# Sums of a router pass in one operation, buffer clearing moved behind the first casts, an inner loop in the overflow path

## The chip, the cores and the metric

One Trainium2 chip, of which the kernel uses one core. The metric is the device time of one execution in microseconds (us); the time of a kernel is the median of several runs. The core has five engines that run side by side, each with its own queue, in order: TensorE (PE, matmul), VectorE (DVE), ScalarE (ACT), GpSimd (POOL) and SyncE (SP, which here only issues transfers). They wait for each other through semaphores. Transfers (DMA) are issued from the queues of SP, ACT and POOL.

## The reference

```python
# attention: q, k, v (8, 8, 576, 64)
scores = q @ k^T / 8
gamma  = 1 - 2 ** (-5 - head)
D      = where(i >= j, gamma ** (i - j), 0)
x      = ((scores * D) @ v)            # -> x (4608, 512)
# mixture of 8 experts, two of them for each of the 4608 rows
noisy  = x @ w_gate + log1p(exp(x @ w_noise)) * noise
top2   = two largest of noisy in each row
w      = exp(l - max(l)) over these two, divided by their sum
out[row] += w * (relu(x[row] @ w1[e]) @ w2[e])   # for both experts e of the row
```

## The kernel before

**Attention.** 16 units (`u`): a unit is four heads of one batch; four units make a pair of batches (`bp`, 0 to 3). The main loop runs `n` from 0 to 16 and works on unit n and, for the outputs, on unit n-1. SP loads q, k and v of unit n+4 at step n (L172, L177); the loads go into buffers that rotate by four. The last 64 rows of both batches of a pair, the tail, are loaded apart (`load_tail`, L184, tile rawt). `cast` scales k and q by the decay tables and turns them into bfloat16 (kn L195, qb L203) and casts v (vn L200, on ACT). Units 0 and 1 are cast by DVE ahead of the loop, all others by POOL, two steps ahead. PE transposes q and k (L245), ACT evicts them (QT, KT L247), PE computes scores (L260), DVE multiplies them by a triangular mask (S L265, St L337 for the tail), PE computes states (T L284, evicted into Tb L290) and outputs (x L310, L318, evicted into xT L324).

**Router.** When a pair of batches is done, `route(bp)` handles its 1152 rows (128 partitions x C = 9 columns). It is a generator: the main loop takes one piece of it between parts of the attention (`step`, `piece`), and this sets the order on every engine's queue, since the whole stage is under a schedule written out by hand. A pass: logits on PE (R L507), softplus on ACT, top two with DVE (L534 to L566: M has a one for each of the two experts, [P, C, 2, E]), then the counts. `thr` (L572, L573) is the capacity of the chosen expert, `py` (L576, L578) its first row in the buffer, each a product with M and a sum over the E experts. PE sums M over the earlier rows (L604 to L612); `prf` adds the base of the earlier pairs (L617). `rk` (L618, L621) is the row's place among the rows of the same expert and slot, `rc` (L623 to L626) among both slots. From these follow the overflow flag `ov` (L642, L643), the payload `pl` that POOL builds (L593 to L598, L627, L644, L645) and copies beside x (L648), from where SP stores x and payload in `xd` (L650); and the list of rows by expert, through one-hot tiles olo and oh (L665 to L672, PE L682) into `xi`. In SP's queue the stores L650 of a pass stand ahead of the loads of the following steps.

**Experts.** `early` (L386 to L411) computes five tiles of 256 rows as soon as two or three pairs are routed, interleaved with the last attention steps and the last routing pass. `experts` does the other 35: gather by indirect DMA (L841), transposes (L948), first matmul (L964), relu (L969, L971), second matmul (L984), then the first expert's weighted rows to `yd` (L1015), and the sum with them to `out` (L1025, scatter L1031). `load_weights` (L1094, L1097) loads the first two experts' weights through POOL's queue at steps 11 to 14.

**Overflow.** Rows beyond an expert's capacity are handled in `overflow`, a loop that runs `nov` times, a number computed on the chip; all engines load it (L752) and branch (L753). Its body finds the rows of a block with 72 one-hot tiles `oh` (L773) and 72 matmuls into `pL` (L774), written out one after the other.

**Head.** DVE clears the four Tb tiles (L163), sets the constants ones, ltri, mask, maskt (L56 to L85, which POOL then cuts to triangles), copies iota and local into PSUM (L452, L454) and clears base and atleast, all ahead of its first cast.

Of the kernel before, what the change touches and what calls it, by code (L numbers as in the profile page):

```python
# [10 lines left out]
F32 = mybir.dt.float32  # L11
BF16 = mybir.dt.bfloat16
I32 = mybir.dt.int32
AX = mybir.AxisListType.X
Alu = mybir.AluOpType
Act = mybir.ActivationFunctionType

P = 128
N = 4608
NCOL = N // P  # L20
E = 8
# [7 lines left out]
HPE = CAP // P  # L29
# [15 lines left out]
HD = 64  # L45
# [5 lines left out]
def constants(nc, cp):  # L51
    K = {}
    K["ident"] = cp.tile([P, P], BF16, name="ident")
    make_identity(nc, K["ident"])
    K["ones"] = cp.tile([P, P], BF16, name="ones")
    nc.vector.memset(K["ones"], 1.0)  # L56
    K["ltri"] = cp.tile([P, P], BF16, name="ltri")
    nc.vector.memset(K["ltri"], 1.0)
    nc.gpsimd.affine_select(K["ltri"], K["ltri"], pattern=[[1, P]], base=0, channel_multiplier=-1,
                            compare_op=Alu.is_gt, fill=0.0)  # L60
# [12 lines left out]

    K["mask"] = cp.tile([P, 2, P], BF16, name="mask")
    nc.vector.memset(K["mask"], 1.0)
    for h in range(2):
        for rs in range(2):
            m = K["mask"][h * HD:(h + 1) * HD, rs, :].rearrange("p (r q) -> p r q", r=4)
            nc.gpsimd.affine_select(m, m, pattern=[[1, 4], [4, 32]], base=-rs, channel_multiplier=-2,
                                    compare_op=Alu.is_ge, fill=0.0)  # L80
    K["maskt"] = cp.tile([P, 2, HD], BF16, name="maskt")
    nc.vector.memset(K["maskt"], 0.0)
    for b in range(2):
        m = K["maskt"][b * HD:(b + 1) * HD, b, :]
        nc.vector.memset(m, 1.0)  # L85
        nc.gpsimd.affine_select(m, m, pattern=[[1, HD]], base=0, channel_multiplier=-1,
                                compare_op=Alu.is_ge, fill=0.0)
# [5 lines left out]
    for h in range(2):  # L93
        t = K["tok"][h * HD:(h + 1) * HD]
# [38 lines left out]
class Attention:  # L133
# [26 lines left out]
    def tables(self):  # L160
        self.kg, self.qg, self.tg = decay_tables(self.nc, self.cp, self.bf)
        for t in self.Tb:
            self.nc.vector.memset(t, 0.0)  # L163
# [23 lines left out]

    def cast(self, u, eng=None):

        nc = self.nc  # L190
        d = self.u[u]
        eng = eng or nc.gpsimd
        hq = self.unit(u)[1]
        kn = self.bf.tile([P, 2, 2, 4, HD], BF16, name="kn", bufs=3)
        eng.tensor_tensor(kn.rearrange("p r c h d -> p (c h) r d"),  # L195
                                d.pop("rawk").rearrange("p c h (r d) -> p (c h) r d", r=2),
                                self.kg[:, hq].rearrange("p c h r -> p (c h) r").unsqueeze(3).to_broadcast(
                                    [P, 8, 2, HD]), Alu.mult)
        vn = self.bf.tile([P, 2, 2, 4, HD], BF16, name="vn", bufs=3)
        nc.scalar.activation(vn.rearrange("p r c h d -> p (c h) r d"),  # L200
                             d.pop("rawv").rearrange("p c h (r d) -> p (c h) r d", r=2), Act.Copy)
        qb = self.bf.tile([P, 4, 4, HD], BF16, name="qb")
        eng.tensor_tensor(qb.rearrange("p r h d -> p h r d"),  # L203
                                d.pop("rawq").rearrange("p c h w -> p (c h w)").rearrange(
                                    "p (h r d) -> p h r d", h=4, r=4),
                                self.qg[:, hq].unsqueeze(3).to_broadcast([P, 4, 4, HD]), Alu.mult)
        d.update(kn=kn, vn=vn, qb=qb)
# [227 lines left out]
class Router:  # L435
    def __init__(self, tc, ctx, K, at, wgn, moe_noise, xd, keep):
        self.tc, self.nc, self.K, self.at = tc, tc.nc, K, at
        self.wgn, self.xd, self.keep = wgn, xd, keep
        nc = self.nc
# [12 lines left out]
        nc.vector.tensor_copy(self.iota, K["iota"])  # L452
        self.local = bank[:, 368:368 + NC9]
        nc.vector.tensor_copy(self.local, K["local"])  # L454

        self.base = self.one.tile([P, 2, E], F32, name="base")
        nc.vector.memset(self.base, 0.0)
        self.atleast = {}
        for n in (2, 3):
            t = self.atleast[n] = self.one.tile([P, 2, E], F32, name=f"atleast{n}")  # L460
# [14 lines left out]
    def route(self, bp):  # L475

        nc, K, sp = self.nc, self.K, self.sp
        V = nc.vector
        ps = self.at.ps
        C = NC9  # L480
# [24 lines left out]
        for c in range(C):  # L505
            for di in range(KD):
                nc.tensor.matmul(pg[:, c].rearrange("p s e -> p (s e)"), lhsT=xcol(c, di),  # L507
                                 rhs=self.wgn[:, di].rearrange("p s e -> p (s e)"), start=(di == 0), stop=(di == KD - 1))
# [15 lines left out]
        def col(name):  # L524
            return sp.tile([P, C], F32, name=name)
# [30 lines left out]
        w = sp.tile([P, 2, C], F32, name="w")  # L556
        V.tensor_tensor(w[:, 0], w1, w2, Alu.max)
        V.tensor_tensor(w[:, 1], w1, w2, Alu.min)
        SH = [P, C, 2, E]
        M = sp.tile(SH, BF16, name="M")  # L560
# [4 lines left out]
        d = col("d")  # L565
# [4 lines left out]
        pd = sp.tile(SH, F32, name="pd", bufs=1)  # L570
        thr = sp.tile([P, C, 2], F32, name="thr")
        V.tensor_mul(pd, M, K["cap"][:, 0:2].unsqueeze(1).to_broadcast(SH))  # L572
        V.tensor_reduce(thr, pd, AX, Alu.add)  # L573
        yield
        row(5)
        V.tensor_mul(pd[:, :, 0], M[:, :, 0], K["cap"][:, 2].unsqueeze(1).to_broadcast([P, C, E]))  # L576
        py = col("py")
        V.tensor_reduce(py, pd[:, :, 0], AX, Alu.add)  # L578
# [13 lines left out]
        G = nc.gpsimd  # L592
# [4 lines left out]
        G.tensor_scalar(pl[:, :, 0], w[:, 1], -1.0, float(E), Alu.mult, Alu.add)  # L597
        G.tensor_copy(pl[:, :, 3], K["tok"][:, bp])  # L598
# [19 lines left out]
        V.tensor_mul(pd, M, prf)  # L618
        yield
        rk = sp.tile([P, C, 2], F32, name="rk")  # L620
        V.tensor_reduce(rk, pd, AX, Alu.add)  # L621
        prs = sp.tile([P, C, E], F32, name="prs", bufs=1)
        V.tensor_add(prs, prf[:, :, 0], prf[:, :, 1])  # L623
        V.tensor_mul(pd, M, prs.unsqueeze(2).to_broadcast(SH))
        rc = sp.tile([P, C, 2], F32, name="rc")
        V.tensor_reduce(rc, pd, AX, Alu.add)  # L626
# [27 lines left out]
        V.tensor_copy(hi, lh[:, 1])  # L654
        e10 = sp.tile([P, 2, C], F32, name="e10")
        V.tensor_scalar(e10, w, -float(HPE), float(HPE * E), Alu.mult, Alu.add)
        V.tensor_add(hi, hi, e10)
# [88 lines left out]
def overflow(tc, K, w1, w2, keep, xd, yd, out):  # L746
# [3 lines left out]
    with tc.tile_pool(name="ov_c", bufs=1) as cp, tc.tile_pool(name="ov_o", bufs=4) as op, \  # L750
         tc.tile_pool(name="ov_ps", bufs=1, space=bass.MemoryType.PSUM) as ps:
        n = nc.values_load(keep["nov2"][0:1, 0:1], min_val=0, max_val=NOV)  # L752
        with tc.For_i(0, n, 1) as iv:  # L753
# [10 lines left out]
            vals = cp.tile([P, 2, NCOL, 3], BF16, name="vals")  # L764
            for j in range(2):
                V.tensor_copy(vals[:, j, :, 0], K["pidx"].to_broadcast([P, NCOL]))
                V.tensor_copy(vals[:, j, :, 1], K["cols"])
                V.memset(vals[:, j, :, 2], float(j))
            pL = ps.tile([P, 3], F32, name="pL")
            for j in range(2):  # L770
                for c in range(NCOL):
                    oh = op.tile([P, P], BF16, name="oh")
                    V.tensor_scalar(oh, K["iota"], rel[:, j, c:c + 1], None, Alu.is_equal)  # L773
                    nc.tensor.matmul(pL, lhsT=oh, rhs=vals[:, j, c, :], start=(j == 0 and c == 0),  # L774
                                     stop=(j == 1 and c == NCOL - 1))
            L = cp.tile([P, 3], F32, name="L")
            V.tensor_copy(L, pL)
# [324 lines left out]
def kernel(  # L1102
# [27 lines left out]
    with ExitStack() as actx, tc.manual_schedule(engines=order):  # L1130
# [38 lines left out]
        at.tr(0, "k")  # L1169
        at.cast(1, nc.vector)  # L1170
        for n in range(NU + 1):
# [101 lines left out]
```

## Time and profile before

| | |
|---|---|
| five runs | 495.59, 496.13, 497.38, 494.50, 493.87 us; median 495.59 |
| profiled execution | 500.35 us, of it the span from the first to the last instruction 498.7 us |
| PE | 412.9 us busy (83%) |
| VectorE | 242.3 us (49%), 642 instructions |
| ScalarE | 275.8 us (55%) |
| GpSimd | 268.6 us (54%), 346 instructions |
| granted PE clock | 0.91 of full speed in the mean |
| DMA | 104.21 MB, 209 GB/s in the mean |

The busy shares are means over stages that differ. Read by stage: up to 54 us the input loads run without a pause and the engines wait for them; from 54 to 171 us attention and three routing passes run on all engines at once; from 171 to 218 us PE does the early expert tiles while the fourth pass runs; from 218.8 to 480.7 us PE does the 35 other tiles, 7.39 us each; the last scatter lands at 485.5, and the rest of the span is the way past the overflow loop and the end of the program. A line of a timeline gives the start in us, the duration in us, engine, line, operation, output<-inputs, shapes, and in brackets the idle time before it and what ended it.

### The profile page before, as it was taken

To read this page: it belongs to the slowest core of one execution; us is meant where nothing else is said; L and a number is where in the kernel's file an instruction comes from. 1 tells how busy PE (TensorE), PEld (TensorE's weight loads), DVE (VectorE), ACT (ScalarE), POOL (GpSimd) and SP (SyncE) were. 2 spreads that over 40 slices of the span, in tenths; PEclk is the share of its full clock that TensorE was granted. 3 is DMA by queue.
4 is the path that set the end of the run, shared out by engine and by line. 5 is a ranking of instruction groups with operands and counts; after the bars stand their busy time and mean duration, and the time that the engine had idled before them with its cause. 6 is when DMAs were issued, how large, how long until landed. Compare 5 with 4: busy or idle time off the path is not lost.

```text
span 498.7 us, 11756 instructions
## 1 busy us (share of the span) xinstructions
PE 412.9 (83%) x4688; PEld 300.1 (60%) x4688; DVE 242.3 (49%) x642; ACT 275.8 (55%) x405; POOL 268.6 (54%) x346
## 2 busy tenths in 40 slices
PE   0763378697677599989999999999999999999950
PEld 0652367576566467657766766766766766766620
DVE  4531068849867729624334444435345445445240
ACT  3770689678658357554657656655655643322200
POOL 3760734834953423485155717637657777776440
PEclk9987597768777899989999999999999999999985
DMA  8999992797795812573786886887978946545330
GB/s 242 284 266 203 273 288 49 222 300 148 207 219 122 185 44 101 172 244 131 253 253 227 270 305 234 295 290 240 332 268 272 338 138 203 170 141 186 111 126 5
DMA packets 92858, 104.21 MB, mean 209 GB/s; under 512 B 22135, under 2 KB 69752, under 8 KB 92800
## 3 DMA queue, kind: packets, MB, share of 16 engines
q1 hardware_dynamic: 77040, 70.04, 47.7%
q0 software_dynamic: 14176, 32.83, 23.1%
q8 instruction: 38, 0.62, 0.5%
q10 hardware_dynamic: 1584, 0.56, 0.4%
q14 instruction: 20, 0.16, 0.1%
HBM read 84.66 MB, written 28.72 MB: 227 GB/s over the span
## 4 chain that ended last, share of the span: by engine, by line
PE 65%; DVE 11%; DMA 7%; SPq 7%; ACT 4%; issue 2%; POOL 1%; POOLq 0%; ACTq 0%; DVEq 0%
PE p L964 25%; PE po L984 24%; DMA raw_v<-in_v_dram 3%; SPq L177 3%; PE pt L948 3%; PE x L405 3%; DVE S L265 3%; PE T L395 2%; PE S L395 2%; SPq L184 1%; DMA raw_k<-in_k_dram 1%; DMA rawt_k<-in_k_dram 1%; DVE olo L665 1%; DMA rawt_v<-in_v_dram 1%; PE S L260 1%
## 5 line engine op out<-in xcount | busy, mean ns | idle before, releaser
L964 PE MATMUL p<-xgT,w 128*128 128x256 bf16 x1120 | 212.9, 275 | 0.0
L984 PE MATMUL po<-w,hT 128*128 128x512 bf16 x560 | 209.8, 379 | 0.0
L964 PEld LDWEIGHTS <-w 128*128 128x128 bf16 x1120 | 110.4, 99 | 71.1
L971 DVE TENSOR_SCALAR hT<-p 128x512 bf16<-128x512 f32 x70 | 48.4, 692 | 148.3 <-PE p L964 148.3
L969 ACT ACTIVATE hT<-p 128x512 bf16<-128x512 f32 x70 | 41.8, 597 | 121.4 <-PE p L964 96.1
L841 POOL DMA_INDIRECT xg<-xd,xi x68 | 68.9, 1014 | 20.2 <-issue 13.0
L1031 POOL DMA_INDIRECT out_dram<-o,ix x45 | 45.6, 1014 | 58.3 <-DVE o L1025 50.7
L265 DVE TENSOR_TENSOR S<-S,mask 128x1024 bf16<-128x1024 f32 x32 | 39.1, 1221 | 52.6 <-PE S L260 52.6
L993 POOL DMA_INDIRECT prv<-yd,ix x45 | 45.1, 1002 | 27.2 <-DMA yd<-y 13.9
L984 PEld LDWEIGHTS <-hT 128*128 128x128 bf16 x560 | 54.8, 98 | 7.5
L914 ACT ACTIVATE w<-wst 128x1024 bf16<-128x1024 f32 x48 | 47.9, 1047 | 0.0
L951 ACT ACTIVATE xgT<-pt 128x1024 bf16<-128x1024 bf16 x35 | 35.6, 1018 | 1.5 <-PE pt L948 1.5
L195 POOL TENSOR_TENSOR kn<-raw_k,kg 128x1024 bf16<-128x1024 f32 x14 | 26.6, 1900 | 17.0 <-PE T L284 8.5
L1025 DVE SCALAR_TENSOR_TENSOR o<-po,g,prv 128x512 f32<-128x512 f32 x45 | 31.6, 742 | 0.8 <-PE po L984 0.8
L260 PE MATMUL S<-QT,KT 64*64 64x128 bf16 x512 | 16.3, 258 | 13.2 <-DVE S L265 7.7
L203 POOL TENSOR_TENSOR qb<-raw_q,qg 128x1024 bf16<-128x1024 f32 x14 | 26.7, 1908 | 0.0
L245 PE MATMUL tr<-ident,qb 128*128 128x128 bf16 x128 | 13.9, 274 | 12.7 <-DVE qb L203 12.7
L200 ACT ACTIVATE vn<-raw_v 128x1024 bf16<-128x1024 f32 x16 | 16.9, 1058 | 11.4 <-DMA raw_v<-in_v_dram 11.4
L290 ACT ACTIVATE Tb<-T 64x512 bf16<-64x512 f32 x32 | 18.9, 590 | 7.1 <-PE T L284 6.7
L284 PE MATMUL T<-vn,kn 64*64 64x64 bf16 (+2 forms) x512 | 22.1, 225 | 0.0
L948 PE MATMUL pt<-ident,xg 128*128 128x128 bf16 x272 | 20.8, 220 | 1.2 <-ACT xgT L951 1.2
L260 PEld LDWEIGHTS <-KT 64*64 64x64 bf16 x512 | 10.8, 126 | 17.3 <-issue 9.2
(215 smaller groups left out, 595.2 us busy)
## 6 DMA issues: line engine op xcount, KB each, us to landing
wst<-in_moe_w_dram SPq DMA_DIRECT2D x48, 512.0 KB, 6.1
raw_k<-in_k_dram SPq DMA_DIRECT2D x32, 256.0 KB, 6.1
raw_v<-in_v_dram SPq DMA_DIRECT2D x32, 256.0 KB, 6.0
yd<-y SPq DMA_DIRECT2D x16, 512.0 KB, 3.6
raw_q<-in_q_dram SPq DMA_DIRECT2D x15, 512.0 KB, 6.4
xd<-xr SPq DMA_DIRECT2D x12, 396.0 KB, 3.4
w<-in_moe_w_dram POOLq DMA_DIRECT2D x4, 1024.0 KB, 11.1
yd<-raw_v SPq DMA_DIRECT2D x5, 512.0 KB, 5.1
```

The source lines that it names most:

```text
L260: nc.tensor.matmul(p[e * HD:(e + 1) * HD, h, 2 * c + r, :], lhsT=d["K"][s, hp, c, r, e, :], rhs=d["Q"][s, hp, 2 * c + e, :], start=(c == 0 ...
L265: nc.vector.tensor_tensor(S.rearrange("p h c r t -> p (h c) (r t)"), p.rearrange("p h (c r) t -> p (h c) (r t)", r=2), self.K["mask"].rear ...
L841: tc.nc.gpsimd.indirect_dma_start(out=xg[:, s, :], out_offset=None, in_=xd[:, :], in_offset=IOff(ap=keep["xi"][:, j:j + 1], axis=0), bound ...
L914: nc.scalar.activation(W[e][:, k * F:(k + 1) * F], t, Act.Copy)
L948: nc.tensor.transpose(pt[:, di, s * P:(s + 1) * P], xb[:, di * P:(di + 1) * P], K["ident"])
L951: return lambda: nc.scalar.activation(xgT, pt, Act.Copy)
L964: nc.tensor.matmul(p1[:, f2, :], lhsT=w[:, o:o + P], rhs=xgT[:, di, :], start=(di == 0), stop=(di == KD - 1))
L969: nc.scalar.activation(hT[:, 2 * fp:2 * fp + 2, :], p1, Act.Relu)
L971: V.tensor_relu(hT[:, 2 * fp:2 * fp + 2, :], p1)
L984: nc.tensor.matmul(po[s], lhsT=hT[:, fi, s * P:(s + 1) * P], rhs=w[:, o:o + DM], start=(fi == 0), stop=(fi == KF - 1))
L993: nc.gpsimd.indirect_dma_start(out=prv[i % NP][:, s, :], out_offset=None, in_=yd[:rows, :], in_offset=IOff(ap=st[i]["ix"][:, s, 1:2], axis=0),
L1031: ins = nc.gpsimd.indirect_dma_start(out=out[:, :], out_offset=IOff(ap=st[i]["ix"][:, s, 0:1], axis=0), in_=st[i]["o"][:, s, :], in_offset ...
```

## The change

Three edits. In the router, four products with M are put side by side in one tile `pd` (capacity, first row, prf, prs), and one sum over the experts (`red`, [P, 4, C, 2]) takes the place of four; three of the products, the sum prs of the two slots, and `e10` are computed by POOL; the copy `hi` is folded into the addition. In the head, the memsets of mask, maskt, ones and ltri go to POOL, in another order; the clearing of Tb goes behind DVE's cast of unit 0; the copies into PSUM and the clearing of base and atleast (`fixed`) go behind DVE's cast of unit 1; the casts of v of units 0 and 1 go behind the evictions of unit 0's transposes in ACT's queue. In the overflow path, the 36 columns of one-hots become an inner loop, with a sum in SBUF.

```diff
 def constants(nc, cp):
+    K["mask"] = cp.tile([P, 2, P], BF16, name="mask")
+    nc.gpsimd.memset(K["mask"], 1.0)
...
+    nc.gpsimd.memset(K["maskt"], 0.0)
...
-    nc.vector.memset(K["mask"], 1.0)
...
+    K["ones"] = cp.tile([P, P], BF16, name="ones")
+    nc.gpsimd.memset(K["ones"], 1.0)
+    K["ltri"] = cp.tile([P, P], BF16, name="ltri")
+    nc.gpsimd.memset(K["ltri"], 1.0)
...
     def tables(self):
         self.kg, self.qg, self.tg = decay_tables(self.nc, self.cp, self.bf)
-        for t in self.Tb:
-            self.nc.vector.memset(t, 0.0)
...
+    def cast_v(self, u):
+        d = self.u[u]
+        vn = d["vn"] = self.bf.tile([P, 2, 2, 4, HD], BF16, name="vn", bufs=3)
+        self.nc.scalar.activation(vn.rearrange("p r c h d -> p (c h) r d"),
+                                  d.pop("rawv").rearrange("p c h (r d) -> p (c h) r d", r=2), Act.Copy)
...
+        if eng is None:
+            self.cast_v(u)
...
+    def fixed(self):
+        nc = self.nc
+        nc.vector.tensor_copy(self.iota, self.K["iota"])
+        nc.vector.tensor_copy(self.local, self.K["local"])
         nc.vector.memset(self.base, 0.0)
...
-        pd = sp.tile(SH, F32, name="pd", bufs=1)
-        thr = sp.tile([P, C, 2], F32, name="thr")
-        V.tensor_mul(pd, M, K["cap"][:, 0:2].unsqueeze(1).to_broadcast(SH))
-        V.tensor_reduce(thr, pd, AX, Alu.add)
+        G = nc.gpsimd
+        pd = sp.tile([P, 4] + SH[1:], F32, name="pd", bufs=1)
+        red = sp.tile([P, 4, C, 2], F32, name="red")
+        G.tensor_tensor(pd[:, 0], M, K["cap"][:, 0:2].unsqueeze(1).to_broadcast(SH), Alu.mult)
+        G.tensor_tensor(pd[:, 1], M, K["cap"][:, 2:3].unsqueeze(1).to_broadcast(SH), Alu.mult)
         yield
         row(5)
-        V.tensor_mul(pd[:, :, 0], M[:, :, 0], K["cap"][:, 2].unsqueeze(1).to_broadcast([P, C, E]))
-        py = col("py")
-        V.tensor_reduce(py, pd[:, :, 0], AX, Alu.add)
...
+        e10 = sp.tile([P, 2, C], F32, name="e10")
+        G.tensor_scalar(e10, w, -float(HPE), float(HPE * E), Alu.mult, Alu.add)
         G.tensor_copy(pl[:, :, 3], K["tok"][:, bp])
...
         V.tensor_tensor(prf, pr, self.base.unsqueeze(1).to_broadcast(SH), Alu.add)
-        V.tensor_mul(pd, M, prf)
-        yield
-        rk = sp.tile([P, C, 2], F32, name="rk")
-        V.tensor_reduce(rk, pd, AX, Alu.add)
         prs = sp.tile([P, C, E], F32, name="prs", bufs=1)
-        V.tensor_add(prs, prf[:, :, 0], prf[:, :, 1])
-        V.tensor_mul(pd, M, prs.unsqueeze(2).to_broadcast(SH))
-        rc = sp.tile([P, C, 2], F32, name="rc")
-        V.tensor_reduce(rc, pd, AX, Alu.add)
+        G.tensor_tensor(prs, prf[:, :, 0], prf[:, :, 1], Alu.add)
+        G.tensor_tensor(pd[:, 3], M, prs.unsqueeze(2).to_broadcast(SH), Alu.mult)
+        V.tensor_mul(pd[:, 2], M, prf)
+        yield
+        V.tensor_reduce(red, pd, AX, Alu.add)
+        thr, py, rk, rc = red[:, 0], red[:, 1, :, 0], red[:, 2], red[:, 3]
         G.tensor_tensor(py, py, rk[:, :, 0], Alu.add)
...
-        V.tensor_copy(hi, lh[:, 1])
-        e10 = sp.tile([P, 2, C], F32, name="e10")
-        V.tensor_scalar(e10, w, -float(HPE), float(HPE * E), Alu.mult, Alu.add)
-        V.tensor_add(hi, hi, e10)
+        V.tensor_add(hi, lh[:, 1], e10)
...
-            pL = ps.tile([P, 3], F32, name="pL")
-            for j in range(2):
-                for c in range(NCOL):
+            L = cp.tile([P, 3], F32, name="L")
+            V.memset(L, 0.0)
+            with tc.For_i(0, NCOL, 1) as ic:
+                relc = op.tile([P, 2, 1], F32, name="relc")
+                V.tensor_copy(relc, rel[:, :, bass.ds(ic, 1)])
+                V.tensor_copy(vals[:, :, 1], K["cols"][:, bass.ds(ic, 1)].to_broadcast([P, 2]))
+                pL = ps.tile([P, 3], F32, name="pL")
+                for j in range(2):
                     oh = op.tile([P, P], BF16, name="oh")
-                    V.tensor_scalar(oh, K["iota"], rel[:, j, c:c + 1], None, Alu.is_equal)
-                    nc.tensor.matmul(pL, lhsT=oh, rhs=vals[:, j, c, :], start=(j == 0 and c == 0),
-                                     stop=(j == 1 and c == NCOL - 1))
-            L = cp.tile([P, 3], F32, name="L")
-            V.tensor_copy(L, pL)
+                    V.tensor_scalar(oh, K["iota"], relc[:, j, :], None, Alu.is_equal)
+                    nc.tensor.matmul(pL, lhsT=oh, rhs=vals[:, j, :], start=(j == 0), stop=(j == 1))
+                V.tensor_add(L, L, pL)
...
         at.tr(0, "q")
         at.tr(0, "k")
+        at.cast_v(0)
+        for t in at.Tb:
+            nc.vector.memset(t, 0.0)
         at.cast(1, nc.vector)
+        at.cast_v(1)
+        rt.fixed()
         for n in range(NU + 1):
```

## The prediction

> **What bounds the kernel now.** I read the chain of waits first, then the waits of the first 60 us, then the busy time by stage, then the timeline of VectorE (DVE) and GpSimd (POOL) around one routing pass, and last the end.
>
> ```profile
> PE 65%; DVE 11%; DMA 7%; SPq 7%; ACT 4%; issue 2%; POOL 1%; POOLq 0%; ACTq 0%; DVEq 0%
> 171.00:191.00 20.00, 19.09 (x204) 14.35 (x204) 6.99 (x30) 11.81 (x19) 2.71 (x4) 0.86 0.36 111
> 191.00:218.70 27.70, 26.69 (x208) 17.86 (x206) 19.16 (x69) 16.62 (x25) 16.27 (x31) 1.00 0.42 135
> ```
>
> The second and third lines are stages (from:to, length, then busy time of PE, weight loads, DVE, ACT, POOL, granted clock, DMA). From 171 us on PE is busy 95% of the time: early expert tiles, then 35 tiles at 7.39 us each (the L948 transposes of the chain start at 226.29, 233.68, 241.07), up to 480.7. So whatever the change does before 171 us ends as one number, the shift of the moment at which PE takes up this work, and a routing pass behind that moment has slack.
>
> ```profile
> ACT vt L217 <- DMA rawt_v<-in_v_dram: 17.0, 2, 15.7
> PE tr L226 <- ACT QT L247: 14.6, 1, 14.6
> ```
>
> These are waits between 28 and 60 us. ACT stands 15.7 us for a load that lands at 54.19, and PE 14.6 us behind it. Up to 54 us the loads are the bound: SP issues them back to back, and no issue waits for a buffer for longer than 0.1 us.
>
> ```profile
> 118.51 1.91 DVE L618 TENSOR_TENSOR pd<-M,prf 128x144 f32<-128x144 bf16 x1
> 121.22 1.05 DVE L623 TENSOR_TENSOR prs<-prf 128x72 f32<-128x72 f32 x1
> 122.31 0.31 DVE L624 TENSOR_TENSOR pd<-M,prs 128x144 f32<-128x144 bf16 x1
> 122.65 0.30 DVE L626 TENSOR_REDUCE rc<-pd 128x18 f32<-128x144 f32 x1
> 118.35 1.91 POOL L195 TENSOR_TENSOR kn<-raw_k,kg 128x1024 bf16<-128x1024 f32 x1
> 120.20 1.97 POOL L203 TENSOR_TENSOR qb<-raw_q,qg 128x1024 bf16<-128x1024 f32 x1
> 122.14 0.20 POOL L627 TENSOR_TENSOR py<-py,rk 128x9 f32<-128x9 f32 x1
> ```
>
> This is pass 1 (pair 1 of four). L618 and L623, which take 0.31 and 0.23 us where POOL is idle (pass 2), end as POOL's kn and qb end. In passes 0 and 1 the sums therefore already end just behind POOL's cast, and DVE is without a gap on the chain from there. Pass 2 (150 to 171) has no cast; pass 3 (183 to 203) lies under PE's work.
>
> **Part 1, the sums.** Removed from DVE, as steps of the chain: the capacity sums L572/L573 0.47 us (114.82 to 115.29), the row sums L576/L578 0.40 (115.71 to 116.11), L621, L623, L624, L626 and, after the sums, L654 and L656 0.18 with a gap. Added on DVE: one sum of 576 elements. Rows of 144 and 768 elements take 0.30 (L626) and 0.95 us (L739), 1.04 ns an element, so 0.75, and 0.67 to the next, which doesn't need it. Added on POOL: two products early (M is ready at 113.6, and POOL idles until 117.2: nothing), e10, and the pair prs and M*prs, which stand in its queue behind the cast. No row has POOL at 144 elements. The nearest:
>
> ```profile
> L711 POOL TENSOR_SCALAR w_all<-w_all 128x72 f32<-128x72 f32 x1 | 0.8, 817 | 0.0
> L713 POOL TENSOR_TENSOR key<-key,ov_all 128x72 f32<-128x72 f32 x1 | 0.8, 765 | 0.0
> L712 POOL TENSOR_TENSOR key<-key,w_all 128x72 f32<-128x72 f32 x1 | 0.3, 344 | 0.0
> L594 POOL TENSOR_TENSOR pl<-d,df 128x9 f32<-128x9 f32 x2 | 0.4, 206 | 15.7 <-DVE df L588 15.7
> ```
>
> Below: 0.20 us (9 elements). Above: 0.82. I take L712's 0.34 for 72 elements and, with 1.58 ns an element from there to L214's 1.04 us at 512, 0.46 for 144; L711 and L713 ran while DVE worked on SBUF tiles of 768 elements, which won't be so here. With 0.08 between dependent operations (L595 to L596) the pair costs 0.34+0.08+0.46 = 0.88 us; e10 costs a pitch of 0.27 (L597 to L598).
>
> Pass 0: capacity sums fall where DVE waits for PE anyway (idle before 77.73), row sums bring df 0.40 earlier; e10 takes 0.27 back, so kn starts 0.13 earlier. qb ends at 84.47; the pair ends at 85.32, the sum is passed at 85.37+0.67 = 86.04. Before, L628 stood at 85.39. So +0.65 for the payload copy L648, on which SP's store and all loads behind it wait, and +0.65-0.18 = +0.47 for the score mask L265, on which PE waits (idle 2.11 before 88.42).
> Pass 1: df is 0.53 earlier (not 0.87: the exponential on ACT ends at 115.60). kn starts at +0.47-0.53+0.27 = +0.21. The pair starts at 122.35, ends 123.23, the sum is passed at 123.95 against L628's 122.95: +1.0. L648 frees SP that much later, and with it the last unit's loads (issued from 129.28, landed 149.82, for which ACT waits 2.43): +1.0 at 150.
> Pass 2: PE's scores end at 156.88, so the mask at 157.13 gains only 0.2. POOL ends the pair at about 159.48 (its six operations start 0.40 earlier, and prs waits for L618); the sum is passed at 160.20 against 160.48, and 0.18 more follows: -0.46. With +1.0 from pass 1 that is +0.54 at 171.
> Pass 3: L501 at 190.85 is 0.5 earlier and PE's idle of 0.29 before 191.32 goes: -0.29. Its late end has cover: the first gather lands at 209.35, PE wants it at 218.76; without that cover its +1 would be on the path.
> **Sum +0.25 us.** With 0.20 for every POOL operation the shift stands by the same steps at +0.07, +0.13 and -0.33 after passes 0, 1 and 2, and ends at -0.6. With 0.82 it stands at +1.9, +3.8 and +4.7, and ends at +4.4.
> *GPSIMD Engine Reference*, section 3.1, is against this part: a tensor_tensor on GpSimd is 1.96 times slower than on VectorE. Estimated from it, the pair costs 1.96 x (0.23+0.31) + 0.08 = 1.14, 0.26 more in each of two passes, and the sum would be +0.8; the 1024-element rows here (1.90 against 1.25) give only 1.5.
>
> **Part 2, the head.** DVE's memsets (6.15 to 10.1) leave its queue ahead of the first cast; kn could start at 7.05 (landing 7.01) and not 10.15. But ACT, which evicts the transposes, is held by its weight load L1140 until 13.5, so QT comes 1.0 earlier (vn, 1.06, now stands behind). POOL gets six memsets and ends its constants before its wait for that load (18.88). In DVE's queue Tb's memsets (2.11) now stand between qb, done by about 9.6, and the second kn, whose data land at 12.16; `fixed` (0.97) then ends by about 15.7, and the mask behind it is wanted at 16.1 at the earliest. The 1 us ends in the waits for rawt_q (POOL, 27.48) and for 54.19 shown above: 0. Without that cover it is worth up to 3.1.
>
> **Part 3, the overflow path.** Its loop runs nov times, and no instruction of its body is in the trace. Order and waits of the main stream stay. What is left is the way past the body:
>
> ```profile
> 482.74 2.73 DMA out_dram<-o,ix
> 485.80 0.18 POOL nov L1085
> ```
>
> The chain ends here, the span at 498.7. The sequencers' records in between show the registers loaded by 486.56, a semaphore operation of POOL (1.94), all other engines through by 490.98, and a POOL drain from 490.76 to 497.86. PE has 133 instructions less to jump over; the drain is POOL's alone. So 0; bounds from 7.1 gained (the drain goes) to 1.9 lost (a second such semaphore operation, should the inner loop bring one on the way past; the exit keeps the same rows).
> *Runtime: NRT & Kernel Launch*, Instruction fetch mechanics, says that a jump outside the two fetched pages stalls for a fetch. By it the shorter body could save an estimated fetch; 16 KB pages take about 1 us in this trace, but under POOL's drain, so the sum stays.
>
> **Sum against the time.** Profiled execution 500.35 (span 498.7 and 1.65 around it) + 0.25 = 500.6. It is 1.0% above the median, 495.59; shifts carry over in us, so **495.8**.
>
> **Rivals.**
> - *POOL in DVE's way* (slower). Price 0.82 for each POOL operation: 495.59+4.4 = 500.0. For it: two of three 72-element rows; in passes 0 and 1 nothing hides POOL. Against: those rows had DVE beside them. It decides from about 0.6 an operation. Chance 0.22.
> - *The head counts* (faster). 495.59-3.1 = 492.5. Against: 15.7 us of idle time between it and the rest. 0.08.
> - *The end gets shorter* (faster). The drain goes with the smaller program: 488.5; half of it, 492. Nothing in the rows ties it to the body. 0.08.
> - *The clock* (faster). The granted clock is 0.5 from 169.7 to 176.5, where eight L395 matmuls take 1.71 instead of 0.87: three such groups and two of L682 lose 2.9 us. If pass 2's gain keeps the clock up: 492.9. Against: 0.46 us of 2.2 idle. 0.10.
>
> **How the numbers follow.** No change: 0.52. The five runs before spread from 493.87 to 497.38, so 0.5% (2.5 us) is about what a measurement can tell from no change. Faster 0.08+0.08+0.10 = 0.26, slower 0.22. The likeliest case alone has -0.6 to somewhat over +1: 494.9 to 497.5 with the runs' spread. The range reaches to the clock and head cases below and most of the way to the POOL case above: 492.6 to 499.2.
>
> **What would show it.** Right: pd<-M,prs on POOL near 0.46, the sum at 0.75 with a DVE wait for POOL just before it in passes 0 and 1; last raw_v landing some 1 us later; rawt_v landing still at 54.2; the same span behind 485.8. Wrong: PE busy before 54 us in a way that moves 54.2, a drain other than 7.1 us, or POOL operations of 0.8 us.

## The result, and the profile after

The changed kernel takes 496.24 us (median of 42 runs, 493.85 to 500.20), the kernel before 496.93 us on the same chips (79 runs, 492.87 to 501.12). The ratio is 0.9999, with a 95% interval from 0.9984 to 1.0014: no difference larger than 0.16%, or 0.8 us. Here and below a ratio is taken over the fast runs of both kernels alone and a median over all runs, some of which are a per cent or more slower, so that a ratio is not the quotient of the two medians. The forecast was 495.8, no change.

The two profiled executions do differ: 500.35 us before (span 498.7), 497.34 after (span 495.3). That is mostly spread from run to run: the profiled execution before is 3.4 us above its kernel's median, the one after 1.1. Of the gap 1.4 us are there when pass 0 makes its M, and most of the rest opens between 87 and 110 us, where the granted clock was at half speed at other times: the stage from 94.60 to 108.20 us has 0.50 before and 1.00 after, the one from 87.80 to 94.70 has 0.99 before and 0.51 after. So in what follows moments of a routing pass are not read from the start of the program, but from the moment at which DVE makes the selection matrix M of that pass (L561 before, L567 after; 113.30 and 109.25 in pass 1). What lies ahead of the pass drops out.

The chain of waits by engine, and the two stages behind 171 us (from:to, length, then busy time of PE, weight loads, DVE, ACT, POOL, granted clock, DMA share, GB/s), of the changed kernel:

```profile
PE 59%; DVE 5%; DMA 4%; ACT 3%; POOL 3%; issue 2%; SPq 1%; POOLq 0%; ACTq 0%
...
171.00:191.00 20.00, 19.09 (x203) 13.62 (x202) 8.57 (x36) 14.14 (x22) 5.07 (x14) 0.95 0.22 74
191.00:218.70 27.70, 25.36 (x201) 17.59 (x200) 16.49 (x53) 14.96 (x23) 18.28 (x30) 0.98 0.53 179
```

PE is still the bound behind 171 us, and still busy 95% of the stage up to 191. The shares of the chain can't be compared with those before: the profile follows this chain back to 106.58 us only, the one before to 0.91. Where it covers pass 1, it runs through POOL's kn, qb, prs and pd into the sum red (114.82 to 120.23 us), where it ran through DVE's pd (L618) and prs (L623) before.

The waits between 28 and 60 us:

```profile
ACT vt L220 <- DMA rawt_v<-in_v_dram: 14.7, 2, 13.8
PE tr L229 <- ACT QT L250: 11.2, 1, 11.2
```

ACT still waits 13.8 us for the last load of the tail. The load landed at 52.98, before at 54.19; but the kernels below without any edit of the head have ACT's vt behind it at 53.34 to 54.41, so this is spread.

Pass 1 on the timeline (start, duration, engine, line, operation, and in brackets the idle time before it and what ended it):

```profile
113.10 0.17 DVE L592 TENSOR_TENSOR df<-df,low 128x9 f32<-128x9 f32 x1
114.78 1.91 POOL L199 TENSOR_TENSOR kn<-raw_k,kg 128x1024 bf16<-128x1024 f32 x1
115.54 1.31 DVE L626 TENSOR_TENSOR pd<-M,prf 128x144 f32<-128x144 bf16 x1
116.64 1.98 POOL L206 TENSOR_TENSOR qb<-raw_q,qg 128x1024 bf16<-128x1024 f32 x1
118.57 0.33 POOL L624 TENSOR_TENSOR prs<-prf 128x72 f32<-128x72 f32 x1
118.98 0.46 POOL L625 TENSOR_TENSOR pd<-M,prs 128x144 f32<-128x144 bf16 x1
119.48 0.75 DVE L628 TENSOR_REDUCE red<-pd 128x72 f32<-128x576 f32 x1 [1.97 <-POOL pd L625]
121.93 1.22 DVE L268 TENSOR_TENSOR S<-S,mask 128x1024 bf16<-128x1024 f32 x1
123.20 0.42 PE L263 MATMUL S<-QT,KT 64*64 64x128 bf16 x16 [2.92 <-DVE S L268]
```

The pair prs and M*prs stands behind the cast in POOL's queue, DVE waits 1.97 us for it, the one sum takes 0.75 us, and PE waits 2.92 us for the score mask L268 that stands behind all this in DVE's queue.

The new operations as groups (count, then busy us and mean ns of one):

```profile
L625 POOL TENSOR_TENSOR pd<-M,prs 128x144 f32<-128x144 bf16 x4 | 1.8, 460 | 0.3
L624 POOL TENSOR_TENSOR prs<-prf 128x72 f32<-128x72 f32 x4 | 1.4, 360 | 0.6 <-DVE prf L622 0.6
L628 DVE TENSOR_REDUCE red<-pd 128x72 f32<-128x576 f32 x4 | 3.0, 750 | 5.7 <-POOL pd L625 5.7
```

DVE is busy 7.3 us less (235.0 instead of 242.3, 600 instructions instead of 642), POOL 6.6 us more (275.2 instead of 268.6), and DVE waits 5.7 us for POOL ahead of the four sums.

The end, from the chain and the timeline:

```profile
479.74 2.73 DMA out_dram<-o,ix
...
482.79 0.19 POOL L1087 COPY nov<-nov 128x1 int32<-128x1 int32 x1 [2.06 <-DMA out_dram<-o,ix]
```

From this copy to the end of the span it is 12.6 us, before 12.9. In the sequencers' records POOL's semaphore operation still takes 1.94 us and its last drain 7.10; what is shorter is the stretch from the load of nov to the drain, 4.41 us instead of 4.74. With the inner loop alone (e_over below) it is 4.74 as well, so these 0.3 us are not shown to come from the loop.

### The profile page after: what moved, and what is told of

Its sections match the earlier page's. It is cut to its first block, busy times and chain, and to the rows that moved or that the text cites. A ratio compares the mean times of both kernels' runs of the same rounds, so it can differ in the third digit from the quotient of the medians.

```text
span 495.3 us, 11741 instructions
## 1 busy us (share of the span) xinstructions
PE 417.6 (84%) x4688; PEld 304.0 (61%) x4688; DVE 235.0 (47%) x600; ACT 275.4 (56%) x405; POOL 275.2 (56%) x372
## 4 chain that ended last, share of the span: by engine, by line
PE 59%; DVE 5%; DMA 4%; ACT 3%; POOL 3%; issue 2%; SPq 1%; POOLq 0%; ACTq 0%
PE p L966 25%; PE po L986 24%; PE pt L950 3%; DMA raw_v<-in_v_dram 3%; PE x L408 2%; PE T L398 1%; PE S L398 1%; DVE olo L665 1%; ACT xr L505 1%; POOL kn L199 1%; DVE oh L672 1%; DVE S L268 1%; DVE oh L669 1%; DMA out_dram<-o,ix 1%; SPq L175 0%
## 5 line engine op out<-in xcount | busy, mean ns | idle before, releaser
L268 DVE TENSOR_TENSOR S<-S,mask 128x1024 bf16<-128x1024 f32 x32 | 39.1, 1222 | 48.5 <-PE S L263 48.5
L263 PE MATMUL S<-QT,KT 64*64 64x128 bf16 x512 | 17.0, 264 | 16.0 <-DVE S L268 8.0
L263 PEld LDWEIGHTS <-KT 64*64 64x64 bf16 x512 | 11.1, 129 | 20.3 <-issue 9.7
L287 PE MATMUL T<-vn,kn 64*64 64x64 bf16 (+2 forms) x512 | 23.1, 230 | 0.0
L250 ACT ACTIVATE QT<-tr 128x1024 bf16<-128x1024 bf16 x16 | 16.4, 1023 | 11.0 <-DMA raw_v<-in_v_dram 8.1
```

The lines of the kernel that those rows point to most:

```text
L268: nc.vector.tensor_tensor(S.rearrange("p h c r t -> p (h c) (r t)"), p.rearrange("p h (c r) t -> p (h c) (r t)", r=2), self.K["mask"].rear ...
```

## The experiments

A ratio is to the kernel before, which ran in turn on the same chip. "M to mask" is the time from M to the score mask behind the sums (L268, for which PE waits), "M to store" to the copy of the payload L651 (which releases SP's stores and the loads behind them).

| kernel | median us | ratio, 95% interval | M to mask, pass 0 / 1 | M to store, pass 0 / 1 |
|---|---|---|---|---|
| before | 496.93 | | 11.92 / 11.63 | 13.90 / 13.60 |
| changed | 496.24 | 0.9999 [0.9984, 1.0014] | 12.60 / 12.68 | 14.87 / 14.95 |
| e_sums | 496.14 | 0.9990 [0.9954, 1.0026] | 12.36 / 12.26 | 14.62 / 14.52 |
| e_head | 496.28 | 0.9993 [0.9959, 1.0028] | 11.58 / 12.52 | 13.56 / 14.48 |
| e_over | 496.53 | 0.9984 [0.9948, 1.0019] | 11.92 / 11.64 | 13.90 / 13.61 |
| e_headlate | 495.90 | 0.9977 [0.9946, 1.0009] | 12.41 / 12.66 | 14.67 / 14.92 |
| e_pool5 | 505.32 | 1.0145 [1.0099, 1.0191] | 14.47 / 14.56 | 16.74 / 16.82 |
| e_pairdve | 496.93 | 0.9991 [0.9956, 1.0026] | 13.28 / 12.88 | 15.54 / 15.14 |
| e_pairfirst | 493.95 | 0.9933 [0.9899, 0.9967] | 11.63 / 10.82 | 13.90 / 13.09 |
| e_qfirst | 492.28 | 0.9893 [0.9850, 0.9937] | 10.09 / 10.59 | 14.22 / 14.72 |
| e_qfirst_again | 544.81 | 0.9963 [0.9929, 0.9997] | 10.10 / 10.58 | 14.23 / 14.71 |
| e_order_only | 547.28 | 0.9968 [0.9920, 1.0016] | 11.18 / 11.13 | 15.03 / 14.96 |
| e_order_only_again | 540.63 | 0.9971 [0.9914, 1.0028] | 11.11 / 11.13 | 14.96 / 14.98 |
| e_noover | 542.90 | 0.9936 [0.9897, 0.9974] | 12.29 / 12.67 | 14.56 / 14.94 |

The medians of the last four stand apart because they ran where the kernel before took 546.98 and 537.31 us; more on that below. M to mask and M to store come from one profiled execution each. The two profiles of e_qfirst agree within 0.01 us and those of e_order_only within 0.07, but the spread is larger: e_head and e_over have the router of the kernel before, e_sums, e_headlate and e_noover that of the changed one, and among equal routers M to mask differs by up to 0.34 us in pass 0 and 0.89 in pass 1. By this spread pass 0 tells the two routers apart (11.58 to 11.92 against 12.29 to 12.60), pass 1 doesn't (11.63 to 12.52 against 12.26 to 12.68).

**One part alone: e_sums, e_head, e_over.** Each is the kernel before with one of the three edits of the diff and nothing else.

> Part 1 of the change alone (sums on one operation, products on GpSimd), on the kernel before. Theory (what VectorE saves is given back by its wait for GpSimd's pair behind the cast): +0.25 us against the kernel before, between -0.6 and +1.5; in passes 0 and 1 the sum of 576 elements at 0.75 us stands behind a VectorE wait of about 2 us for GpSimd's second product, in pass 2 without one. Rival (a loss here is hidden in the whole change by a gain of another part): +2 to +4.4 us. Rival (fewer VectorE operations gain): -1.5 us or more.

> Part 2 of the change alone (clearing of buffers behind the first casts, constants on GpSimd). Theory (the loads bound the time up to 54 us): 0 us within 1; the first kn starts near 7.0 us instead of 10.15, but the transposes of the pair's tail still start near 28.6 us and the load of rawt_v still lands at 53 to 54.2 us. Rival (the head counts): -3.1 us, rawt_v's successor work on ScalarE starting as much earlier.

> Part 3 of the change alone (the inner loop in the overflow path's body, which runs no times on these data). Theory: 0 us within 1; GpSimd's last drain stays 7.1 us and its semaphore operation ahead of it 1.94 us, one of it. Rivals: the drain shortens with the smaller body, -3.5 to -7.1 us; a second such semaphore operation, +1.9 us.

All three are at 0 within their intervals (-0.5 us for the sums, between -2.3 and +1.3; the others alike). No loss of one part is hidden by a gain of another that the runs could see. In e_sums DVE's wait ahead of the sum is 1.96 us in pass 0, 3.56 in pass 1 (DVE did its other work there sooner), none in pass 2. In e_head the first kn starts at 7.12 instead of 10.15 us, the transposes of the tail still at 28.95. In e_over the drain takes 7.10 us and the one semaphore operation 1.94.

**The head's cover, doubled: e_headlate.** The changed kernel with

```diff
+        junk = at.cp.tile([P, DM], F32, name="junk")
+        for _ in range(12):
+            nc.vector.memset(junk, 0.0)
         at.cast(0, nc.vector)
```

> The changed kernel with 12 more VectorE memsets of 512 elements (6.3 us) ahead of the first cast, on a buffer that nothing reads; the first kn starts near 13.3 us instead of 7.0. Theory (the loads bound the time up to 54 us, with 15 us of idle time on ScalarE and TensorE ahead of it): 0 to +0.7 us against the changed kernel, rawt_v still landing at 53 to 54.5 us. Rival (the head counts): +3 to +6.3 us. Rival (the cast frees the raw buffers later and the loads themselves shift): +1 to +3 us, with rawt_v landing that much later.

The memsets took a pitch of 0.66 us each, so the first kn starts at 13.80 us, 6.8 later than in the changed kernel and 3.65 later than in the one before. The time is 495.90 (a ratio of 0.9977; the changed kernel's is 0.9999), and ACT's wait for the load that bounds this stage is as long as ever:

```profile
ACT vt L220 <- DMA rawt_v<-in_v_dram: 14.2, 1, 14.2
```

So 6.8 us of delay at the head cost nothing that the runs can see, and the 3 us that the change gives there are worth nothing. The load landed at 53.70 us, so it did not shift with the cast either.

**POOL's price: e_pool5.** The product M*prs is made five times in the changed kernel:

```diff
-        G.tensor_tensor(pd[:, 3], M, prs.unsqueeze(2).to_broadcast(SH), Alu.mult)
+        for _ in range(5):
+            G.tensor_tensor(pd[:, 3], M, prs.unsqueeze(2).to_broadcast(SH), Alu.mult)
```

> The changed kernel with the product M*prs on GpSimd made five times instead of once (the same result). 4 x 0.43 = 1.72 us more in the pair of each pass. Theory by the prediction's steps (GpSimd's pair is on the path in passes 0 and 1, and in pass 2 but for 0.2 us of slack, and pass 3 has cover): +3.2 to +5 us against the changed kernel, VectorE's wait 3.7 us in passes 0 and 1. Rival (a wait there is taken up by the loads behind it): under +1.7 us.

Pass 1 on its timeline:

```profile
123.31 0.33 POOL L624 TENSOR_TENSOR prs<-prf 128x72 f32<-128x72 f32 x1
123.72 2.62 POOL L626 TENSOR_TENSOR pd<-M,prs 128x144 f32<-128x144 bf16 x5
126.37 0.75 DVE L629 TENSOR_REDUCE red<-pd 128x72 f32<-128x576 f32 x1 [5.71 <-POOL pd L626]
```

Five products on one tile took 2.62 us, a pitch of 0.54 and not 0.43, so the dose was about 2.15 us a pass and 6.4 in three. M to mask grew by 1.87 and 1.88 us against the changed kernel in passes 0 and 1. The time grew by 7.2 us against the kernel before (between 4.9 and 9.5). In pass 2 too DVE now waits for POOL (2.24 us), and M to mask is 2.97 us longer there. So what is added to POOL's pair lies on the path in each pass ahead of 171 us: the rival that the loads take up such a wait falls. The expectation was right in the mechanism and low in the numbers: it had 1.72 us a pass, 5.2 in three, and a DVE wait of 3.7 us where 5.71 was measured.

**The pair back on DVE: e_pairdve.**

```diff
-        G.tensor_tensor(prs, prf[:, :, 0], prf[:, :, 1], Alu.add)
-        G.tensor_tensor(pd[:, 3], M, prs.unsqueeze(2).to_broadcast(SH), Alu.mult)
         V.tensor_mul(pd[:, 2], M, prf)
+        V.tensor_tensor(prs, prf[:, :, 0], prf[:, :, 1], Alu.add)
+        V.tensor_tensor(pd[:, 3], M, prs.unsqueeze(2).to_broadcast(SH), Alu.mult)
```

> The changed kernel with the pair prs and M*prs on VectorE, as in the kernel before, and all else as changed. Theory (in passes 0 and 1 VectorE's own pair ends with GpSimd's cast anyway, so GpSimd's pair costs 0.88 us there, twice): -0.5 to -1.2 us against the changed kernel, no VectorE wait for GpSimd ahead of the sum, but pd and prs at 1 to 1.9 us each in passes 0 and 1. Rival (the pair's engine is all that matters and its cost is real): -2 us or more. Rival (no effect at the end): 0 within 0.3 us.

The expected gain did not show. The time can't settle it: -0.4 us against the kernel before, between -2.2 and +1.3. But M to mask did not shorten; it grew by 0.68 and 0.20 us, of which the second is within the spread. The products did as expected. Pass 1:

```profile
115.87 1.96 POOL L199 TENSOR_TENSOR kn<-raw_k,kg 128x1024 bf16<-128x1024 f32 x1
116.00 1.93 DVE L625 TENSOR_TENSOR prs<-prf 128x72 f32<-128x72 f32 x1
117.80 1.90 POOL L206 TENSOR_TENSOR qb<-raw_q,qg 128x1024 bf16<-128x1024 f32 x1
117.96 1.90 DVE L626 TENSOR_TENSOR pd<-M,prs 128x144 f32<-128x144 bf16 x1
120.44 0.74 DVE L628 TENSOR_REDUCE red<-pd 128x72 f32<-128x576 f32 x1
```

One is held to the end of kn, the next to the end of qb, and then St and the sum follow. With the pair on POOL, DVE does St, the masked scores of the tail, while it waits. PE's waits say the same: between 60 and 171 us it waits 3.9 us for the mask S instead of 7.6, but 5.4 for St instead of 1.1, together 9.3 and 8.7. So the pair on DVE, beside the cast, costs no less than the 0.88 us that POOL needs for it behind the cast.

**The pair ahead of the cast: e_pairfirst.** In the main loop of the changed kernel:

```diff
             if u + 2 < NU:
-                at.cast(u + 2)
+                at.cast_v(u + 2)
             if u + 1 < NU:
                 at.tr(u + 1, "k")
             step()
+            if u + 2 < NU:
+                at.cast(u + 2, nc.gpsimd)
```

> The changed kernel with GpSimd's part of the cast (kn, qb) issued one step later, so that the pair prs and M*prs stands ahead of it in GpSimd's queue; the copy of v on ScalarE stays where it was. Theory (VectorE's 1.96 us of wait in passes 0 and 1 is the pair's place behind the cast, and TensorE's idle 2.67 and 2.92 us there hang on it): the wait falls under 0.5 us, the score mask of passes 0 and 1 comes 1 to 1.8 us earlier relative to the mask before it, and the time falls by 2 to 3.5 us against the changed kernel, so -2 to -3.5 against the kernel before. Rival (the loads set the pace between the passes, TensorE's wait there costs nothing): 0 within 1 us though the wait is gone. Rival (the later cast is late for the next transposes): +1 us or more, with TensorE waiting for qb or kn.

493.95 us, 3.3 less than the kernel before (between 1.6 and 5.0). DVE's wait ahead of the sum is gone in passes 0 and 1, and the waits of PE's scores L263 for the mask between 60 and 171 us fall from 7.6 to 4.8 us. The mask of pass 0 came only 0.97 us earlier, though, and the timeline of pass 0 shows why:

```profile
83.66 1.90 POOL L199 TENSOR_TENSOR kn<-raw_k,kg 128x1024 bf16<-128x1024 f32 x1
83.73 0.75 DVE L628 TENSOR_REDUCE red<-pd 128x72 f32<-128x576 f32 x1
85.22 0.37 DVE L638 CAST rki<-red 128x9 int32<-128x9 f32 x1
85.50 0.16 DVE L639 TENSOR_SCALAR rki<-red 128x9 int32<-128x9 f32 x1
85.52 1.90 POOL L206 TENSOR_TENSOR qb<-raw_q,qg 128x1024 bf16<-128x1024 f32 x1
85.69 1.76 DVE L641 TENSOR_SCALAR lh<-rki 128x18 int32<-128x18 int32 x1
```

The sum of 576 elements runs beside kn in its usual 0.75 us, but lh, 18 elements, starts just behind qb's start and takes 1.76 us, to qb's end; in the changed kernel it takes 0.18. The wait has become a hold. *SBUF — State Buffer*, section "Who interferes with whom", says that VectorE and GpSimd share a pair of ports as an exclusive lock, that casts, tensor_scalar and operations with two SBUF inputs can need it, and that tensor_reduce never does on this chip; these rows agree with it.

**The cast cut in two: e_qfirst.** qb stays at its new place, kn goes one piece of the router further, behind the work on ov (`cast_v` stands where `cast` stood, as in e_pairfirst):

```diff
             step()
+            if u + 2 < NU:
+                at.cast_q(u + 2)
...
                 pend.append(rt.route(bp))
             step()
+            if u + 2 < NU:
+                at.cast_k(u + 2)
```

> As e_pairfirst, but the cast is cut in two: qb stands behind the pair, kn only behind GpSimd's operations on ov, so that VectorE's small operations rki, lh and ov don't run beside kn. In e_pairfirst lh took 1.76 us in pass 0 and rki 1.60 in pass 1, ending as GpSimd's qb ended, where both take 0.17 alone. Theory (these two are on the path to the score mask, for which TensorE waits 1.33 and up to 1.6 us): they fall to 0.2 us, TensorE's wait for qb (0.77) goes too, and the time falls by a further 1 to 2.5 us: -4 to -5.5 us against the kernel before. Rivals: kn is late for its transposes, and TensorE's wait for kn gives it back (0 against e_pairfirst); the lock follows to other operations (0).

492.28 us, 5.3 less than the kernel before (between 3.1 and 7.5): this version beats both kernels. That it beats e_pairfirst (between 1.6 and 5.0) is not shown. Pass 1:

```profile
114.94 0.46 POOL L645 TENSOR_TENSOR pd<-M,prs 128x144 f32<-128x144 bf16 x1
115.36 1.90 POOL L197 TENSOR_TENSOR qb<-raw_q,qg 128x1024 bf16<-128x1024 f32 x1
115.44 0.75 DVE L648 TENSOR_REDUCE red<-pd 128x72 f32<-128x576 f32 x1
117.81 0.18 DVE L661 TENSOR_SCALAR lh<-rki 128x18 int32<-128x18 int32 x1
118.67 1.22 DVE L288 TENSOR_TENSOR S<-S,mask 128x1024 bf16<-128x1024 f32 x1
118.95 1.90 POOL L207 TENSOR_TENSOR kn<-raw_k,kg 128x1024 bf16<-128x1024 f32 x1
```

lh is at 0.18 us again, and the mask starts before kn does. The waits of PE's scores for the mask fall further, to 3.3 us. PE now waits 1.1 us for kn in two places, as the first rival said, and its wait for St, 0.4 us in e_pairfirst, is 2.7. The second rival holds in part as well: an addition of 16 elements (L653) behind the sum now takes 0.99 us, to the end of qb, where it took 0.20 in the changed kernel. The store comes 0.3 and 1.1 us later than in the kernel before, and it does not show in the time.

**The same order without the change: e_order_only.** The kernel before, all sums on DVE, with the cut cast of e_qfirst.

> The kernel before, with nothing of the change, and with the cut cast of e_qfirst: qb one step later, kn behind GpSimd's operations on ov. All sums stay on VectorE. Theory (what e_qfirst gains comes from two places: the pair ahead of the cast, which needs the pair on GpSimd, and kn out of the way of rki, lh and ov, which doesn't): one of VectorE's two-input products still waits for qb (1.3 to 1.9 us in passes 0 and 1), the second no longer for kn or qb; -2 to -4 us against the kernel before, 1 to 3 us slower than e_qfirst. Rival (the order alone does it, and the change has no part in it): -5 us, as e_qfirst. Rival (without the pair on GpSimd the order gains nothing): 0 within 1 us.

> e_qfirst once more, for a narrower interval and beside e_order_only on one chip: -4 to -6 us against the kernel before.

> e_order_only once more, since on the chip of its first run the expert tiles took longer than on the others (546.98 us for the kernel before instead of 497), which left e_order_only and e_qfirst within each other's intervals. Theory (the pair ahead of the cast needs the pair on GpSimd): -2 to -4 us against the kernel before, less than the 5 us that e_qfirst gained. Rival (the order alone does it): -5 us. Rival (nothing without the pair on GpSimd): 0 within 1 us.

These runs, and e_noover, were on another chip, where the expert tiles are slower: in e_qfirst_again the tiles keep their 7.39 us up to 265 us, and behind that 11 of 26 take between 7.8 and 20.1 us, with PE waits that the trace puts down to "issue". The stage from 300 to 400 us of e_qfirst and of e_qfirst_again:

```profile
300.00:400.00 100.00, 99.32 (x744) 69.50 (x755) 43.63 (x118) 58.71 (x76) 64.52 (x65) 1.00 0.80 272
```

```profile
300.00:400.00 100.00, 89.89 (x641) 59.74 (x651) 34.31 (x97) 50.39 (x65) 52.80 (x53) 0.97 0.72 235
```

What slows these tiles was not found; no edit touches them. Against the kernel before on that chip, e_qfirst gains 2.0 us (between 0.2 and 3.9), e_order_only 1.8 (between 4.4 gained and 0.9 lost), and once more 1.6 (between 4.6 gained and 1.5 lost). So e_qfirst_again missed its expectation of 4 to 6 us: the gain is there again, but smaller, and why is open. By time e_order_only can be told neither from e_qfirst nor from the kernel before, so none of its three readings falls: the 5 us of the rival that the order alone does it lie outside both intervals, but e_qfirst itself gains only 2.0 us on that chip.

The profiles differ more clearly. In M to mask e_order_only gains 0.74 and 0.50 us on the kernel before, e_qfirst 1.83 and 1.04; the difference between the two is beyond the spread in pass 0 alone. And PE's waits between 60 and 171 us for what DVE masks, S and St together, are 8.7 us in the kernel before (7.3 and 1.4), 8.7 in the changed one (7.6 and 1.1), 7.8 to 8.7 in e_sums, e_head, e_over and e_headlate, and 7.7 (2.6 and 5.1) and 9.9 in the two profiles of e_order_only, but 5.2 in e_pairfirst and 6.0 and 6.1 in the two of e_qfirst. With the order alone PE mostly waits for St in place of S. In pass 1 of e_order_only one product of DVE is held by qb:

```profile
114.78 1.91 POOL L199 TENSOR_TENSOR qb<-raw_q,qg 128x1024 bf16<-128x1024 f32 x1
114.94 1.91 DVE L644 TENSOR_TENSOR pd<-M,prf 128x144 f32<-128x144 bf16 x1
117.65 0.22 DVE L649 TENSOR_TENSOR prs<-prf 128x72 f32<-128x72 f32 x1
```

That is the theory's picture: the pair on POOL takes a wait away that the order alone only moves. Whether it is worth the 1 to 3 us stays open.

**The end without the loop: e_noover.** The call of `overflow` is taken out of the changed kernel, so the overflow path is left out.

> The changed kernel with the overflow path left out (its loop runs no times on these data; the program has no loop at its end). Theory (GpSimd's drain of 7.1 us sets the end and isn't tied to the body): the drain stays near 7.1 us, and only the register load, the semaphore operation of 1.94 us and the branches go: -3 to -5 us against the changed kernel (out_dram's last landing at 2.7 us behind its issue, the drain starting at once behind it instead of 4.6 us behind nov's copy). Rival (the drain belongs to the loop or to the program's size): -7 to -12 us, with a drain under 1 us.

The sequencers' records have POOL's drain from 529.22 for 7.32 us, 0.3 us behind the landing of the last scatter. From that scatter's issue to the end of the span it is 11.1 us, in the changed kernel 15.6: the loop's way past costs 4.5 us, and the drain doesn't belong to the loop. The time fell by 3.5 us against the kernel before on that chip (between 1.4 and 5.6); the changed kernel, to which the expectation compares, was not run there.

## Why the prediction was right, step by step

**The bound.** As read: loads up to 54 us, PE from 171 us on. e_headlate added 6.8 us of delay ahead of 54 us without an effect that the runs can see, e_pool5 added about 6.4 us between 54 and 171, and the time grew by 7.2 (between 4.9 and 9.5).

**Part 1, the prices.** POOL's 144 elements took 0.46 us and its 72 elements 0.33 (0.45 in pass 2), against 0.46 and 0.34 taken from far rows; the sum 0.75 against 0.75. The rival "POOL in DVE's way" with 0.82 an operation fell with these rows. The two rows that spoke for it, L711 and L713, still take 0.8 us in the changed kernel: their size does not make it. The prediction counted them as two of three rows of 72 elements; there is a fourth, L714, at 0.41 us. *GPSIMD Engine Reference*, section 3.1, with its factor of 1.96, which it gives for 2048 elements, was too dear here: 0.46 against DVE's 0.31 (L624 before), 0.33 against 0.23, so 1.4 to 1.5.

**Part 1, pass 0.** Forecast +0.65 on the store and +0.47 on the mask, measured +0.97 and +0.68 (e_sums +0.72 and +0.44). The mechanism held. What was too hopeful is df, which was to come 0.40 earlier and came 0.17 earlier after M. And L628 was read 0.08 us too late in all three passes: it starts at 85.31, 122.87 and 160.40, so the same working gives +0.73, +1.08 and -0.38.

**Part 1, pass 1.** Forecast +1.0 at the store, measured +1.35 (e_sums +0.92; e_head, with the router of the kernel before, +0.88, so the spread is nearly as large). Again df: forecast 0.53 earlier, measured 0.19 later (e_sums 0.21 earlier): the xr copy ahead of it in DVE's queue started only at 111.82, 1.05 us after DVE had become idle, as PE's transposes for it ended (111.10 to 111.73). Then a step that did not show, *"with it the last unit's loads ... +1.0 at 150"*: the last raw_v is issued 1.33 us later after M (20.53 instead of 19.20), but lands only 0.27 later (36.79 instead of 36.52). In e_sums it is issued 0.97 later and lands 0.05 later; in e_pool5 3.55 and 3.59. But e_head, with the router of the kernel before, also has it 1.10 later and landing 1.14 later (20.30 and 37.66), so a shift of 1 us is within the spread of single profiles. The time from issue to landing is 15.8 to 17.4 us in these profiles, and what sets it stays open. So the +1.0 is neither shown nor refuted; that the sum came out near 0 may owe something to luck here.

**Part 1, passes 2 and 3.** Pass 2: forecast -0.46, the mask is 0.64 earlier after M (e_sums 0.16 later); no wait for POOL in it, as said. M to mask is 12.31 to 13.37 us there with the router of the kernel before and 10.00 to 12.47 with that of the changed one, so a gain of half a us can't be read from it. Pass 3: not foreseen was that DVE waits for POOL there too, 1.81 us before 191.45. It has the cover that the step named: PE's waits from 171 to 219 us add up to 3.1 us, before to 4.0.

**The sum** of +0.25 us can't be told from the measured -0.05 (between -0.8 and +0.7). That it is near 0 through two things that cancel, DVE's savings and DVE's wait, is shown for the wait: a longer one costs time (e_pool5), and with the pair ahead of the cast the time falls by 3.3 us (e_pairfirst, though there kn and qb move too). The savings were not measured by a run of their own. That PE waits 8.7 us for DVE's masks in both kernels fits the two cancelling.

**Part 2, the head.** Forecast 0, with kn at 7.05 and QT 1.0 earlier because of ACT's weight load. Measured: kn at 6.99, ACT's first QT at 14.0 instead of 14.5, so 0.5 earlier and not 1.0, the tail's transposes at 28.66 instead of 28.58. The cover was larger than the 3.1 us that the step needed: e_headlate's first kn starts 3.65 us later than in the kernel before and 6.8 later than in the changed one, at no cost that shows. The rival "the head counts" fell with e_head and e_headlate.

**Part 3, the overflow path.** Forecast 0. e_over is at 0, the drain at 7.10 and the semaphore operation at 1.94 us in both. The rival "the end gets shorter" fell twice: in e_over, and in e_noover, where the loop is gone and the drain stays at 7.32.

**The clock** did not settle into another pattern that could be told from the runs' spread; the half-speed windows stand elsewhere in each profile. This rival was not tested by itself.

## What to carry to other kernels

Work taken from a busy engine is no gain if the engine then waits for it behind a long operation in another queue: look first at what stands ahead of the moved work there, since here the version with the moved work ahead was 3.3 to 5.3 us faster where the kernel takes 497 and 2.0 where it takes 547, and the change itself brought nothing. How much of that the order would give without the moved work, the runs don't tell (1.8 and 1.6 us, neither clear of 0). Where VectorE and GpSimd work on SBUF at once, put VectorE's short two-input operations, casts and tensor_scalars outside of GpSimd's long ones, and let sums fall beside them. To compare moments across profiles whose clock differs, count from an event inside the same stage.

## What the runs showed of the hardware that was not expected

A cast of 9 elements (rki) took 1.60 us on VectorE in pass 1 of e_pairfirst, and a tensor_scalar of 18 elements 1.76 us in pass 0, each up to the end of GpSimd's product of 1024 elements; alone they take 0.16 to 0.18. The prediction had seen this only for products with two inputs.

The kernel before took 497 us in the runs on one chip (6 in the record) and 537 to 547 in those on another (5). Between the two profiles of e_qfirst lie 52.9 us, of which 3.7 are there when the first of the 35 late expert tiles starts (214.78 against 211.11); the rest comes behind 265 us, with a granted clock of 0.97 instead of 1.00 from 300 to 400 us, which doesn't explain it.

GpSimd's last drain takes 7.1 to 7.3 us with or without a loop at the end.
